# Mamba2 and feed-forward kernel: loads, scores and weight pieces of the first scan in another order

## The chip, the cores and the metric

The kernel runs on one core of one Trainium2 chip. The metric is the device time of one execution in microseconds (us), as a median of runs. Beside it stands one profiled execution with a trace of every instruction. Engines are named as in the profile: PE is TensorE's products and PEld its weight loads, DVE is VectorE, ACT is ScalarE, POOL is GpSimd, SP is SyncE, which issues most DMAs.

## The reference

A Mamba2 block over 4 batches, 8 heads, 768 positions, head size 32 and state size 16 comes first; its output, taken as 3,072 tokens of 256 values, goes through a feed-forward layer of 2,048 units.

```python
log_a = log(clip(a, 1e-6, 1))
state = 0
for c in chunks:                       # of 32 positions
    cum = cumsum(log_a[c])
    L = exp(cum[i] - cum[j]) * (i >= j)
    y = ((C @ B.T) * L) @ x + (C @ state) * exp(cum)
    state = exp(sum(log_a[c])) * state + sum_j(B_j x_j * exp(cum[-1] - cum_j))
...
h = y @ w_in                           # 3072x256 by 256x2048
out = (h * sigmoid(1.702 * h)) @ w_out # 2048x256
```

The weights w_in and w_out arrive as 64-bit floats, the other inputs as 32-bit floats.

## The kernel before, in words

Tokens go in six groups of 512. The scan works on pairs of heads and blocks of 128 positions, each split into two halves of 64. The instruction order of every engine is the order in which the program writes them: a function at the end of the program chains each engine's instructions, so nothing is rescheduled. What is written earlier on an engine runs earlier on it and holds up what follows.

**The first scan** (lines 1133 to 1199) makes the first token group. Its chain is: idle products that keep TensorE occupied (`keep_busy`, L437), masks (L545), differences of the running sums of log a (`cum`, L340 and L342, into `ab`, L551), their exponentials (L572), transposed B (`b`, L624), scores C·B (`cb`, L677, one call for each of two pairs), fanned decay rows (`rows`, L509) and their exponentials (`since`, L514), weighing the scores (L688), the state's increments (`A`, L708), `drop` (L519), the increments scaled into `steps` (L727), one scan over them on VectorE (L732), the copied state `S` (L737), then y from scores (L820) and from the state (L808), and the copy of y into the feed-forward's operand (L837). `score` calls `since_first` between its two pairs.

**Selector tiles** are made by GpSimd at the start: `same` (from which `part` is reduced), `pick`, and `whose`, which `rows` multiplies with `cum`. ACT loads a table for Ln, makes `cum` (L340), and loads the next table.

**The hidden layer of group 0** is 16 products `h` (L876), f=0 to f=15, each of two steps over 256 inputs and 512 tokens, and the profile shows 4 records of 0.43 us spacing for each f. Each needs the decoded weights of its tile f. Then come `o` products (L974) of the output layer, and from group 1 on a Strassen-like scheme (X, Y, acc).

**The weight pieces.** Weights are loaded as raw 64-bit words and decoded in `PIECES`: w_in in pieces of 2, 2, 2, 2, 4 and 4 tiles f (numbers 0 to 5), then w_out in four pieces of 4 tiles (6 to 9). `fetch(i)` issues two DMAs on SP for piece i (L180); with `held`, a one-column VectorE write (L171) makes it wait in VectorE's order. Decoding is a row of steps:

- `fields`: two VectorE operations (L192 power, L195 mantissa) on the high words
- `clamp`: two ACT operations (L203, L204) on the power
- `rounded`: one VectorE operation (L208) that adds the low words
- `join`: two VectorE operations (L219 sign into the power, L225 the product, written into `w_in` or `w_out`)

`narrow(i)` is `rounded(i)`, `fields(i+1)`, `join(i)`. A dictionary of places says after which hidden or output product a step stands: in the hidden layer of group 0 `narrow` stands at places 1, 2, 4, 6, 9, 12 for pieces 2 to 7 and the following `clamp` at 1, 2, 4, 7, 12, 15.

**Loads at the start.** On ACT's queue: two of a, four of C. On SP's: two of a, four of B, then the two of piece 0 (256 KB each), then four of x. Pieces 1 to 5 are issued after the first weighing.

**Later scans.** Two further scans stand in the output products of group 0 (place 9) and in the first step of group 1 ("H0"). There `keep_both` multiplies the increments with `part` on VectorE (L755), four operations per place.

Of the kernel before, what the change touches and what calls it, by code (L numbers as in the profile page):

```python
# [35 lines left out]
def kernel(  # L36
# [121 lines left out]
    bits, pieces = {}, {}  # L158
# [4 lines left out]
    def fetch(i, held=False):  # L163
        name, f, n = PIECES[i]
        if n == 2 and f % 4:
            t = pieces.pop(i - 1)[:, 2 * n * DM:]
        else:
            t = pieces[i] = words(f"bits{i}")
            t = t[:, :2 * n * DM]
        if held:  # L170
            nc.vector.memset(t[:, :1], 0)  # L171
        if name == "in":
            src = moe_w_in[:, 2 * f * P:2 * (f + n) * P].rearrange("(k p) e -> p k e", p=P)
            dst, src = (v.rearrange(s, h=n, e=2 * P) for v, s in (
                (t, "p (h k e) -> k p h e"), (src, "p k (h e) -> k p h e")))
        else:
            src = moe_w_out[f * P:(f + n) * P, :].rearrange("(f p) (h e) -> h p f e", p=P, h=2)
            dst = t.rearrange("p (h f e) -> h p f e", h=2, f=n)
        for k in range(2):
            nc.sync.dma_start(out=dst[k], in_=src[k])  # L180
        t = t.rearrange("p (e w) -> p e w", w=2)
        bits[i] = t[:, :, 0], t[:, :, 1]
# [5 lines left out]
    def fields(i):  # L188
        hi, cols = bits[i][1], slice(0, PIECES[i][2] * DM)
        mantissa[i] = wide.tile([P, PN], U32, tag="m", name=f"m{i}")[:, cols]  # L190
        power[i] = wide.tile([P, PN], U32, tag="p2", name=f"p2{i}")[:, cols]
        nc.vector.tensor_scalar(out=power[i], in0=hi, scalar1=0x7FF00000, scalar2=None,  # L192
                                op0=ALU.bitwise_and)

        nc.vector.tensor_scalar(out=mantissa[i], in0=hi, scalar1=0x000FFFFF,  # L195
                                scalar2=0x00100000, op0=ALU.bitwise_and, op1=ALU.bitwise_or)
# [18 lines left out]
    def join(i):  # L215

        name, f, n = PIECES[i]
        hi, m, p2 = bits.pop(i)[1], mantissa.pop(i), power.pop(i)
        nc.vector.scalar_tensor_tensor(out=p2, in0=hi, scalar=0x80000000, in1=p2,  # L219
                                       op0=ALU.bitwise_and, op1=ALU.bitwise_or)  # L220
        if name == "in":
            dst, h = w_in[:, f:f + n].rearrange("p f k e -> p (f k e)").unsqueeze(1), 1
        else:
            dst, h = w_out[:, :, f:f + n].rearrange("p c f e -> p c (f e)"), 2
        nc.vector.scalar_tensor_tensor(  # L225
            out=dst, in0=m.bitcast(FP32).rearrange("p (h e) -> p h e", h=h),
            scalar=2.0 ** -20, in1=p2.bitcast(FP32).rearrange("p (h e) -> p h e", h=h),
            op0=ALU.mult, op1=ALU.mult)
        for n in NEXT.get(i, ()):
            fetch(n)  # L230

    def narrow(i):
        rounded(i)
        if i + 1 < len(PIECES):
            fields(i + 1)
        join(i)
# [48 lines left out]
    load_first("C", [nc.scalar] * R)  # L285
    load_first("B", [nc.sync] * R)
    fetch(0)
    load(0, "x")
    load(1, "x")

# [39 lines left out]
    def fold_ident(k, engine=nc.vector):  # L330
# [8 lines left out]
                            op1=ALU.min)  # L339
    nc.scalar.activation(cum, az0, AF.Ln)  # L340
# [16 lines left out]
    def pick_a(p):  # L357
# [8 lines left out]
    same = ssd.tile([P, NH, D], FP32, tag="BT", name="same")  # L366
    nc.gpsimd.memset(same, 1.0)
    nc.gpsimd.affine_select(
        out=same, in_=same, pattern=[[-N, NH], [0, D]], compare_op=ALU.is_ge,
        fill=0.0, base=0, channel_multiplier=1)  # L370
    nc.gpsimd.affine_select(
        out=same, in_=same, pattern=[[N, NH], [0, D]], compare_op=ALU.is_ge,
        fill=0.0, base=N - 1, channel_multiplier=-1)
    pick = picker("pick", NB, 1, NH)
    whose = const.tile([32 * PG, 1 + PG, NH, N], FP32, name="whose")
    nc.gpsimd.memset(whose, 1.0)
    for i, n, head in ((0, 1, PG), (1, 2, PG), (0, 0, 1)):
        t = whose[32 * i:32 * i + 32, n:n + 1]
        nc.gpsimd.affine_select(out=t, in_=t, pattern=[[-1, 1], [-head, NH], [0, N]],
                                compare_op=ALU.is_equal, fill=0.0, base=-max(n - 1, 0),  # L380
                                channel_multiplier=1)

    part = const.tile([P, Q], FP32, name="part")
    nc.vector.tensor_reduce(
        out=part, in_=same[:, :, 0].rearrange("p (r q) -> p q r", q=Q), op=ALU.add, axis=AX.X)
# [275 lines left out]
    def score(pairs, between=lambda: None):  # L664

        cb = area(f"cb{pairs[0]}").rearrange("p r (k e) -> p r k e", k=2 * PG)
        for n, p in enumerate(pairs):
            s = st[p]
            BT, CT = s["BT"], s.pop("CT")
            s["cb"] = cb[:, :, 2 * n:2 * n + 2]  # L670
            if n:
                between()
            for k in range(2):
                for i, side in enumerate(SIDES):
                    for r in range(R):
                        rows = slice(32 * r, 32 * r + 32)
                        nc.tensor.matmul(  # L677
                            out=s["cb"][side, r, k].rearrange("p (q i) -> p q i", q=Q),
                            lhsT=BT[rows, k, side], rhs=CT[rows, k, :, side],
                            start=True, stop=True, tile_position=(32 * r, H * i),  # L680
                            skip_group_check=True)
# [57 lines left out]
    def keep_both(pairs):  # L739

        for p in pairs:
            part_of(p, range(4))
        for p in pairs:
            add_up(p, range(4))

    def part_of(p, ms):
# [4 lines left out]
        for i in range(2):  # L751
            ks = [m // 2 for m in ms if m % 2 == i]
            if ks:
                k, n = ks[0], len(ks)
                nc.vector.tensor_tensor(  # L755
                    out=new.rearrange("p (k s) (q d) -> p s k q d", s=2, q=Q)[:, i, k:k + n],
                    in0=increment[p][i][:, k:k + n].rearrange("p k (q d) -> p k q d", q=Q),
                    in1=part.unsqueeze(1).unsqueeze(3).to_broadcast([P, n, Q, D]),
                    op=ALU.mult)
# [392 lines left out]
    keep_busy(5, 0)  # L1152
# [3 lines left out]
    for r in range(R):  # L1156
        if r == R - 1:
            pads(0, busy)
# [11 lines left out]
    fields(0)  # L1170
    ends_first(0)
    ends_first(1)
    rounded(0)
    score(range(PG), since_first)
    weigh(0)
    fetch(1, held=True)
    for i in range(2, 6):
        fetch(i)
    rows_a(az, (nc.sync,))
    weigh(1)  # L1180
    drops()
    gain(range(PG))
    parts_first()
    for p in range(PG):
        since_start(p, nc.gpsimd)
    clamp(0)
# [3 lines left out]
    dense(0)  # L1190
    join(0)
    fields(1)
    clamp(1)
    table(AF.Silu)
    rounded(1)
    fields(2)
    clamp(2)
    join(1)
# [18 lines left out]
    for i, k, c in ((2, 1, 1), (3, 2, 2), (4, 4, 4), (5, 6, 7), (6, 9, 12), (7, 12, 15)):  # L1217
# [11 lines left out]
    at(in_project[0], 9, lambda: gain(pairs), lambda: score(pairs), lambda: keep_both(pairs),  # L1229
# [14 lines left out]
       lambda: since_start(n + 1), lambda: gain(later), lambda: score(later),  # L1244
       lambda: keep_both(later), lambda: weigh(n), lambda: weigh(n + 1))
# [186 lines left out]
```

## Time and profile before

| What | Value |
| --- | --- |
| Median of four runs | 351.76 us (351.21 to 352.29) |
| Profiled execution | 350.64 us |
| Its span, first to last instruction | 348.8 us |
| PE busy in the span | 342.8 us |
| DVE busy | 255.1 us |
| ACT busy | 149.8 us |
| POOL busy | 13.0 us |
| Start of the first hidden product | 18.08 us |
| Start of the hidden product f=8 | 33.16 us |

All times in the views are microseconds from the start of the span; the profiled execution is 1.84 us longer than its span. A line of the timeline gives the start, the time to the end of the last of a group, the engine, the line, the operation with its tiles and shapes, and in brackets how long the engine had been idle and what ended that. A line of the waits gives who waited for what, the sum, the number of times and the longest. In the chain of waits, each line is a step of the work that ended last, followed back from the end.

### The profile page before, as it was taken

Reading aid. Unit: us, or ns where it says so; the run is one execution under the profiler, and the core shown is the slowest. Engines: PE = TensorE matmul, PEld = TensorE weight load, DVE = VectorE, ACT = ScalarE, POOL = GpSimd, SP = SyncE. Lnnn points to the kernel's source line nnn. Section 1 sums busy time; section 2 is a strip of 40 time slices with the busy share of each in tenths; the row PEclk is TensorE's granted clock in tenths of the full one; section 3 lists DMA queues with packets and bytes.
Section 4 is the critical chain, followed back from the end, with each engine's and each line's share of the span. In section 5 each row is a group of like instructions: output and inputs, shape, how many; then the busy total and the mean of one; then the engine's idle time right before and its main releaser. Section 6 shows DMA issues by size and latency. Waiting matters only on the chain.

```text
span 348.8 us, 8109 instructions
## 1 busy us (share of the span) xinstructions
PE 342.8 (98%) x3386; PEld 274.0 (79%) x3386; DVE 255.1 (73%) x481; ACT 149.8 (43%) x334; POOL 13.0 (4%) x41
## 2 busy tenths in 40 slices
PE   8899999999999999999999999999999999999996
PEld 6643444548888888888888888888888888899996
DVE  5889999899679998739996548788454654455463
ACT  4798584005354323744342544432554321554320
POOL 8300000100000100000000000000000000000000
PEclk9999999999999999999999999999999999999999
DMA  5599899453627200435503026300000300000301
GB/s 156 121 323 217 236 204 200 85 92 66 112 54 139 45 0 9 70 89 114 103 23 54 2 75 123 62 0 3 0 4 2 60 3 0 0 2 0 62 0 61
DMA packets 89980, 25.92 MB, mean 74 GB/s; under 512 B 73432, under 2 KB 87128, under 8 KB 89944
## 3 DMA queue, kind: packets, MB, share of 16 engines
q1 hardware_dynamic: 89112, 24.88, 33.2%
q10 hardware_dynamic: 832, 0.52, 0.5%
q8 instruction: 26, 0.43, 0.5%
q14 instruction: 10, 0.08, 0.1%
HBM read 22.15 MB, written 3.24 MB: 73 GB/s over the span
## 4 chain that ended last, share of the span: by engine, by line
PE 92%; DMA 3%; DVE 2%; SPq 1%; issue 0%; ACT 0%; DVEq 0%
PE acc L1037 28%; PE X L932 19%; PE Y L942 14%; PE o L974 8%; PE acc L1044 7%; PE h L876 6%; DMA bits<-in_moe_w_in_dram 3%; PE y L820 2%; PE cb L677 2%; PE y L808 1%; SPq L180 1%; PE A L708 1%; PE busy L437 1%; PE ab L551 1%; PE ab L545 0%; DVE c L1068 0%
## 5 line engine op out<-in xcount | busy, mean ns | idle before, releaser
L937 ACT ACTIVATE ac<-X 128x256 f32<-128x256 f32 x76 | 29.1, 383 | 78.6 <-PE X L932 78.2
L1037 PE MATMUL acc<-mg,mw 128*128 128x256 f32 x192 | 54.5, 379 | 0.0
L909 ACT ACTIVATE gT<-gT 128x512 f32<-128x512 f32 (+1 forms) x76 | 39.3, 520 | 33.7 <-DVE gT L1064 33.1
L1064 DVE TENSOR_TENSOR gT<-Y,ac 128x512 f32<-128x512 f32 x38 | 26.2, 689 | 35.7 <-PE Y L942 30.4
L932 PE MATMUL X<-my,mi 128*128 128x256 f32 x152 | 45.1, 380 | 0.0
L1064 DVE TENSOR_TENSOR gT<-Y,b 128x256 f32<-128x256 f32 x38 | 15.9, 419 | 34.8 <-PE Y L942 34.8
L1037 PEld LDWEIGHTS acc<-mg,mw 128*128 128x128 f32 x192 | 36.5, 190 | 5.0
L876 PE MATMUL h<-yT,w_in 128*128 128x512 f32 (+2 forms) x108 | 35.9, 486 | 0.8 <-DVE w_in L225 0.8
L1037 PE MATMUL acc<-gT,w_out 128*128 128x256 f32 x128 | 35.5, 379 | 0.0
L876 PEld LDWEIGHTS h<-yT,w_in 128*128 128x128 f32 x108 | 18.2, 190 | 17.0 <-issue 13.9
L932 PEld LDWEIGHTS X<-my,mi 128*128 128x128 f32 x152 | 28.0, 190 | 3.8 <-ACT ac L937 0.2
L974 PE MATMUL o<-gT,w_out 128*128 128x512 f32 x64 | 28.6, 597 | 0.0
L900 DVE TENSOR_TENSOR mg<-gT 128x512 f32<-128x512 f32 x40 | 27.3, 681 | 0.0
L1037 PEld LDWEIGHTS acc<-gT,w_out 128*128 128x128 f32 x128 | 24.2, 190 | 3.4 <-ACT yT L847 0.2
L937 ACT ACTIVATE b<-X 128x256 f32<-128x256 f32 x38 | 14.6, 384 | 20.3 <-PE X L932 19.8
L932 PE MATMUL X<-yT,w_in 128*128 128x256 f32 x76 | 23.2, 389 | 0.0
L942 PE MATMUL Y<-my,mi 128*128 128x256 f32 x76 | 22.7, 381 | 0.1
L942 PE MATMUL Y<-yT,w_in 128*128 128x256 f32 x76 | 22.7, 381 | 0.0
L932 PE MATMUL X<-my,w_in 128*128 128x256 f32 x76 | 22.5, 379 | 0.0
L942 PE MATMUL Y<-yT,mi 128*128 128x256 f32 x76 | 22.4, 379 | 0.0
L974 PEld LDWEIGHTS o<-gT,w_out 128*128 128x128 f32 x64 | 11.8, 190 | 13.2 <-issue 12.8
L399 DVE TENSOR_TENSOR_SCAN L<-a,idents 128x1024 f32<-128x1024 f32 x9 | 20.5, 2277 | 0.2 <-DMA a<-scratch 0.2
(152 smaller groups left out, 543.8 us busy)
## 6 DMA issues: line engine op xcount, KB each, us to landing
a<-scratch SPq DMA_DIRECT2D x18, 256.0 KB, 5.0
bits<-in_moe_w_out_dram SPq DMA_DIRECT2D x8, 512.0 KB, 5.2
x<-in_x_dram SPq DMA_DIRECT2D x24, 128.0 KB, 3.6
out_dram<-ob SPq DMA_DIRECT2D x40, 64.0 KB, 1.9
bits<-in_moe_w_in_dram SPq DMA_DIRECT2D x8, 256.0 KB, 4.1
bits<-in_moe_w_in_dram SPq DMA_DIRECT2D x4, 512.0 KB, 9.9
b<-in_B_dram SPq DMA_DIRECT2D x20, 64.0 KB, 2.5
af<-in_a_dram SPq DMA_DIRECT2D x3, 384.0 KB
```

What stands on the lines that cost most here:

```text
L399: nc.vector.tensor_tensor_scan(out=L, data0=ra[p].rearrange("p k e -> p (k e)"), data1=idents.rearrange("p h i -> p (h i)"), initial=0.0, ...
L677: nc.tensor.matmul(out=s["cb"][side, r, k].rearrange("p (q i) -> p q i", q=Q), lhsT=BT[rows, k, side], rhs=CT[rows, k, :, side], start=Tru ...
L876: nc.tensor.matmul(out=h[:, cols], lhsT=w_in[:, f, k], rhs=yT[g][:, k, cols], start=(k == 0 and e == 0), stop=(k == NK - 1), skip_group_ch ...
L900: nc.vector.tensor_tensor(out=t[:, 0:2], in0=B[:, :, 1], in1=B[:, 0], op=ALU.subtract)
L909: nc.scalar.activation(o, i, AF.Silu, scale=GELU_SCALE)
L932: nc.tensor.matmul(out=s["X"], lhsT=lhsT, rhs=rhs, start=i == "1", stop=i == "4", skip_group_check=True)
L937: nc.scalar.activation(copy, s["X"], AF.Copy)
L942: nc.tensor.matmul(out=o, lhsT=lhsT, rhs=rhs, start=s.pop("new", False), stop=i != "5", skip_group_check=True)
L974: nc.tensor.matmul(out=o[c], lhsT=w_out[:, c, f], rhs=gT[g, f // 2][:, f % 2], start=(f == 0), stop=(f == NF - 1), skip_group_check=True)
L1037: nc.tensor.matmul(out=acc[g][0][i][:, cols], lhsT=w, rhs=h[:, cols], start=(j == 0 and k == 0 and (i, 0) in begins), stop=(j == NF // 2 - ...
L1044: nc.tensor.matmul(out=o[k] if type(o) is list else o[:, cols], lhsT=h[:, cols], rhs=w, start=(j == 0 and (i, k) in begins), stop=(j == NF ...
L1064: nc.vector.tensor_tensor(out=o, in0=v, in1=w, op=ALU.add)
```

## The change

In the first scan C's loads alternate between SP and ACT and stand ahead of B's; x's loads stand ahead of piece 0. `keep_busy` issues three products instead of five, and two small products stand before the last mask. `whose` is copied from the identity by ACT ahead of `cum`'s Ln; `same` shrinks to one column per head, and `pick` is made later. The two scores stand back to back and `since_first` comes after them and the first weighing. `fields(0)` stands behind the second weighing and ahead of the scan; `rounded(0)` stands behind the state.

Pieces 0 and 1 share one raw tile as before; `fetch(2, both=True)` loads pieces 2 and 3 by two DMAs of 512 KB. `join` can be done in parts: pieces 0, 1 and 4 are joined in two halves, and `fields(1)` is split into its two operations around the second half of `join(0)`. `clamp(6)` moves from place 7 to 8. In the later scans `keep_both` runs on ACT by eight activations per place, and `score` stands ahead of `gain` (place 9) or behind `keep_both` ("H0").

```diff
-    def fetch(i, held=False):
+    def fetch(i, held=False, both=False):
         name, f, n = PIECES[i]
-        if n == 2 and f % 4:
-            t = pieces.pop(i - 1)[:, 2 * n * DM:]
-        else:
-            t = pieces[i] = words(f"bits{i}")
-            t = t[:, :2 * n * DM]
+        n = n * (1 + both)
+        t = half.pop() if half else words(f"bits{i}")
+        if i == 0:
+            half.append(t[:, PN:])
+            t = t[:, :PN]
...
-    def fields(i):
+    def fields(i, steps=range(2)):
...
-    def join(i):
+    def join(i, parts=1, part=None):
+        for k in range(parts) if part is None else (part,):
+            name, f, n = PIECES[i]
+            n //= parts
+            f += k * n
+            cols = slice(k * n * DM, (k + 1) * n * DM)
+            hi, m, p2 = (v[:, cols] for v in (bits[i][1], mantissa[i], power[i]))
...
     def narrow(i):
         rounded(i)
         if i + 1 < len(PIECES):
             fields(i + 1)
-        join(i)
+        join(i, 2 if i == 4 else 1)
...
-    load_first("C", [nc.scalar] * R)
+    load_first("C", [nc.sync, nc.scalar] * PG)
     load_first("B", [nc.sync] * R)
-    fetch(0)
     load(0, "x")
     load(1, "x")
+    fetch(0)
...
+    whose = const.tile([32 * PG, 1 + PG, NH, N], FP32, name="whose")
+    for i, n, head in ((0, 1, PG), (1, 2, PG), (0, 0, 1)):
+        e = 32 * i + max(n - 1, 0)
+        nc.scalar.copy(whose[32 * i:32 * i + 32, n],
+                       ident[32 * i:32 * i + 32, e:e + head * NH:head].unsqueeze(2).to_broadcast(
+                           [32, NH, N]))
     nc.scalar.activation(cum, az0, AF.Ln)
...
-    same = ssd.tile([P, NH, D], FP32, tag="BT", name="same")
+    same = const.tile([P, NH], FP32, name="same")
...
-    pick = picker("pick", NB, 1, NH)
-    whose = const.tile([32 * PG, 1 + PG, NH, N], FP32, name="whose")
-    nc.gpsimd.memset(whose, 1.0)
...
+                if by_scalar:
+                    for q in range(Q):
+                        nc.scalar.activation(o[:, :, q], a[:, :, q], AF.Copy, scale=part[:, q:q + 1])
+                else:
+                    nc.vector.tensor_tensor(
...
-    keep_busy(5, 0)
+    keep_busy(3, 0)
...
-            pads(0, busy)
+            pads(2, busy)
...
-    fields(0)
     ends_first(0)
     ends_first(1)
-    rounded(0)
-    score(range(PG), since_first)
+    score(range(PG))
     weigh(0)
+    since_first()
     fetch(1, held=True)
-    for i in range(2, 6):
+    fetch(2, both=True)
+    for i in range(4, 6):
         fetch(i)
     rows_a(az, (nc.sync,))
     weigh(1)
+    fields(0)
     drops()
     gain(range(PG))
     parts_first()
     for p in range(PG):
         since_start(p, nc.gpsimd)
+    pick = picker("pick", NB, 1, NH)
     clamp(0)
     keep_first()
     dense(2)
     finish(range(PG))
-    dense(0)
-    join(0)
-    fields(1)
+    rounded(0)
+    join(0, 2, 0)
+    fields(1, (0,))
     clamp(1)
+    join(0, 2, 1)
+    fields(1, (1,))
     table(AF.Silu)
     rounded(1)
+    join(1, 2, 0)
     fields(2)
     clamp(2)
-    join(1)
+    join(1, 2, 1)
     load(PG)
...
-    for i, k, c in ((2, 1, 1), (3, 2, 2), (4, 4, 4), (5, 6, 7), (6, 9, 12), (7, 12, 15)):
+    for i, k, c in ((2, 1, 1), (3, 2, 2), (4, 4, 4), (5, 6, 8), (6, 9, 12), (7, 12, 15)):
...
-    at(in_project[0], 9, lambda: gain(pairs), lambda: score(pairs), lambda: keep_both(pairs),
+    at(in_project[0], 9, lambda: score(pairs), lambda: gain(pairs), lambda: keep_both(pairs, True),
        lambda: weigh(PG), lambda: weigh(PG + 1))
...
-       lambda: since_start(n + 1), lambda: gain(later), lambda: score(later),
-       lambda: keep_both(later), lambda: weigh(n), lambda: weigh(n + 1))
+       lambda: since_start(n + 1), lambda: gain(later), lambda: keep_both(later, True), lambda: score(later),
+       lambda: weigh(n), lambda: weigh(n + 1))
```

## The prediction, made before the run

> **What bounds the kernel now.** I read the page's busy shares first, then TensorE's waits over the first 60 us, then the chain of waits from the start, then the timelines of each engine up to 50 us.
>
> ```profile
> PE 342.8 (98%) x3386; PEld 274.0 (79%) x3386; DVE 255.1 (73%) x481; ACT 149.8 (43%) x334; POOL 13.0 (4%) x41
> ```
>
> TensorE is busy for 98%, so only its idle time, and work taken off it, can pay. The list of its waits is short:
>
> ```profile
> PE busy L437 <- DVE ones L296: 1.2, 1, 1.2
> PE h L876 <- DVE w_in L225: 0.8, 1, 0.8
> PE b L624 <- ACT L L572: 0.5, 1, 0.5
> PE y L808 <- DVE S L737: 0.4, 1, 0.4
> ```
>
> The columns are microseconds, times, longest. The last long one is `h` L876 on `w_in` L225. It ends at 33.16, and after it the same list, asked for 50 us to the end, is empty: TensorE runs product against product. So whatever the change gains or loses up to 33.16 moves the whole remaining stream, and nothing later can give it back. The chain up to that point:
>
> ```profile
> 12.34 1.26 DVE L L688 x2
> ...
> 18.40 10.81 DMA bits<-in_moe_w_in_dram
> 29.33 0.69 DVE p L192
> 30.02 0.60 DVE m L195
> 30.62 1.14 DVE p L219
> 31.79 1.24 DVE w_in L225
> 33.16 3.67 PE h L876 x8
> ```
>
> Columns: start, time, what. Hidden product f=8 waits for the first w_in piece of four tiles, and VectorE decodes that (L192 to L225) in one unbroken row. The third view is the front of the timeline (start, time, engine, line, shapes, in brackets the idle time ahead):
>
> ```profile
> 1.21 3.56 PE L437 MATMUL busy<-ones 128*128 128x192 f32 x10 [1.21 <-DVE ones L296]
> 4.44 0.42 ACT L340 ACTIVATE cum<-az 128x256 f32<-128x256 f32 x1 [0.79 <-DVE az L338]
> 4.89 0.69 DVE L342 TENSOR_TENSOR_SCAN cum<-carry,cum 128x256 f32<-128x256 f32 x1 [0.48 <-ACT cum L340]
> 6.41 0.90 PE L551 MATMUL ab<-cum,pick 32*64 32x128 f32 x32
> 7.90 0.69 PE L551 MATMUL ab<-cum,pick 32*64 32x128 f32 x32
> 11.64 0.66 ACT L514 ACTIVATE since<-rows 128x256 f32<-128x256 f32 x2 [1.17 <-PE rows L509]
> 14.62 1.23 DVE L732 TENSOR_TENSOR_SCAN steps<-drop,steps 128x512 f32<-128x512 f32 x1
> 18.08 14.23 PE L876 MATMUL h<-yT,w_in 128*128 128x512 f32 x32
> ```
>
> `cum` is ready at 5.58, but L551, which uses it, starts at 6.41: until then TensorE is still in its idle products and the masks. From there run `ab`, `b`, the scores, `rows`, `since`, drops, the scan at 14.62, and y; the hidden layer starts at 18.08, which is 2.23 after the scan ends.
>
> **The change, part by part.**
>
> *Fewer idle products.* Five become three, 10 records become 6. Spacing is 0.32, so the masks end about 1.28 earlier, near 5.2 (two tiny new pads among them cost no more than 0.1). L551 then waits for `cum`: 5.58 plus about 0.07 is 5.65, which is 0.76 earlier. The same 32 products take 0.90 at 6.41 and 0.69 at 7.90, and single starts lie 0.21 apart before 6.92 and 0.11 after. If that change of pace stays at 6.92, 0.76 us at half pace is worth about 0.47 later: `b`, at 9.70, goes to about 9.23. It follows ACT's L572, whose first bank follows the products and moves with them.
>
> *Selectors.* Three ScalarE copies stand ahead of `cum`'s Ln. No row shows a 32x128 copy; L727's 128x128 steps are 0.25 apart, L737's 128x256 copy takes 0.66. At 0.14 to 0.27 each they take 0.4 to 0.8 from 3.65 on, where ACT is idle 0.79: they end at 4.05 to 4.45 against 4.44. That costs 0 to 0.1, which I take as 0. POOL loses L376/L379, the large `same` and `pick` from its early row; its products CT (7.80) only gain slack.
>
> *Loads.* C now shares SP and ACT, so the four B issues on SP are joined by two of C, but the two bits issues leave: ahead of x stand two issues where two stood. x starts near 5.47 as before, and x (from L708 at 12.16) is not late. B's last issue ends near 5.45 instead of 4.45; with the 2.2 to 2.7 of its landings before it is there by 7.7 to 8.1, and its transpose (L612, 1.02) ends by 8.7 to 9.1, just ahead of `b` at 9.23: cover 0.1, and what lacks there delays all that follows. Piece 0's bits go behind x; that is rival A.
>
> *Scores together, rows after them.* Now `rows` L509 runs after the second score. `since` came 1.94 after `b` (11.64 − 9.70); it now comes after 0.59 + 0.49 + 0.57 + 0.73 = 2.38 (b, two scores, rows to ACT). With `b` at 9.23 that is 11.61, against 11.64: what the front gains, this order takes back. So the scan stays at 14.6 and h starts at 18.05, 0.03 earlier. L688 (weigh), which needs both scores, moves from 12.34 to about 11.07 and ends its second half at 13.42; the held fetch, released by it, moves from 13.62 to about 12.3.
>
> *Fields(0), clamp(0), rounded(0).* Before, fields(0) stood at 9.08 and L208 at 11.14, beside the scan's chain. Now L192/L195 stand between weigh(1) and the scan, and L208 behind S. They take 0.77, so 13.34 to 14.1, inside the 0.5 that VectorE has before 14.62. Cost 0, if the bits have landed by 13.85.
>
> *Decode in halves.* This is the real gain. From h's start TensorE itself needs 0.53 + 31 × 0.43 = 13.86 to f=8: 31.94. It got there at 33.16, so 1.22 is wait (0.23 of it at f=2, about 1.0 at f=8). VectorE's row from S to piece 4 decides. Its steps from start to start are: 512 columns 0.34, 0.34, 0.60 to 0.72, 0.72, 0.61; 1,024 columns 0.60, 0.60, 1.12, 1.25, 1.14; for a half join of 256 columns I go by L1064's 128x256 (0.42 long): 0.45 to the dependent second step, 0.34 to the next. Adding up from S at 15.88: rounded(0) 16.19, half 0 of piece 0 at 17.66 (f=0 needs it at 18.05), half 1 at 18.79 (f=1: 19.9), piece 1's first half at 20.97 (f=2: 21.62, before 21.63), its second 22.44 (f=3: 23.3), piece 2 at 25.05 (f=4: 25.06), piece 3 at 28.2 (f=6: 28.7), first half of piece 4 at 31.84. With the 0.14 from ready to product and some restart at f=4, f=8 runs at 32.15. That is 33.16 − 32.15 = 1.01. Bounds: 0.7 if each half costs 0.1 more and f=4 waits 0.2; 1.22 if no wait is left.
>
> *Pieces 2 and 3 in one load.* Eight issues on SP instead of ten, 0.47 to 0.59 each, starting 1.3 earlier. But piece 2 now needs the whole megabyte. Before, both pieces had landed by 21.85; 1.3 earlier is 20.5, wanted by fields(2) at 20.9: cover 0.4. Piece 4 is wanted at 25.6 (landed by 25.3 before), piece 5 at 29.2 (29.20 before). If the cover goes, its lateness moves f=4 one for one.
>
> *After 33 us.* keep_both goes to ScalarE: eight activations per place instead of four VectorE products of 0.81; ACT is 43% busy and waits for PE there, S has 3.2 to 3.4 cover (70.65 against L808 at 73.87), and Be of pair 5 (84.60 against 85.34) gains VectorE time. Score ahead of gain only swaps TensorE work. clamp(6) at f=8 has its piece ready 2.0 us before its product (46.95 against 48.96), less the 1.0 that TensorE comes earlier and 0.3 for the split join. Cost 0 each; without these covers the first would cost 0.8 per place.
>
> Sum: 0.03 + 1.01 = 1.04 less, out of 350.64 (span 348.8 and 1.84 around it). The median of the runs is 351.76, so 1.12 above the profiled one; the same difference gives 350.7.
>
> **The rivals.**
>
> *A, slower: the scan waits for piece 0.* fields(0) stands ahead of the scan on VectorE, and its bits are now queued behind x, issued until 10.72 (or 9.8, without the 0.94 of bits issues ahead). Its second transfer is issued at 10.3 to 11.2. Piece 1's pair, issued at 13.62 and 14.03, landed 2.8 and 3.9 later; the page's median for a 512 KB bits load is 5.2. So it lands between 13.1 and 16.4, wanted by 13.85. Behind the wait queue scan, S, y and the whole hidden layer, one for one. Landing at 14.9 eats the gain; landing after 15.95 is slower by over 0.3%. Against: the nearest rows, 2.8 to 3.9, end at 15.1, 352.0. For: x goes in small packets (the page counts 73,432 of 89,980 under 512 B) on the same engines just ahead. Its far end, 2.55 late, gives 353.3; I put it at 16.0, 352.9.
>
> *B, the pace of TensorE rises later.* Fewer idle products leave it resting about 0.45 before L551. If the spacing halves only after the scores, L551's second half, b and scores pay up to 1.4; with the order above up to 0.4 of the sum of 1.04 remains: 351.4. For: the pace changed 5.7 us after the first idle product. Against: the granted clock reads 1.00 in every stretch from 1.2 to 100, and the rest is short.
> On this the Trainium skill, "TensorE: Matmul & The Clock Gate", Part 1, says that the clock doubles after a busy window of about 3.4 us that runs freely, not after a number of products; that speaks against taking busy work away. An estimate by that page puts a missed window at up to half of 3.4, 1.7 us later, and the time at 352.4; the trace shows the halved spacing, but not what sets it.
>
> *C, better.* The pace rises earlier, or `rows` slips in sooner, so that the scan starts 0.4 earlier, and the halves end all waits: 1.22 + 0.4 gives 350.1.
>
> *D, it doesn't bite.* Merged pieces 2 and 3, or 4, land late and the wait only moves from f=8 to f=4: gain 0 to 0.4, 351.5.
>
> **How the numbers follow.** The main case has 0.48, A 0.17, B 0.09, C 0.18, D 0.08. A measurement can tell about 0.3%, which is 1.06 us: faster means below 350.7, on which the main case sits, so half of it (0.24) counts as faster, the rest as same. Faster: 0.24, 0.18 of C, and 0.01 each of B and D: 0.44. Slower: 0.12 of A, 0.02 of B: 0.14. Same: 0.42. The range takes C from 349.9 on and reaches up through B and D and the nearer part of A, to 352.4; 0.14 lies above, 0.05 below.
>
> **What would show it.** L551 at 5.6 to 5.7; the scan at 14.5 to 14.7; h starting within 0.1 of 18.05; no wait on `w_in` over 0.2 at f=8, and f=8 at 32.1 to 32.2; then the same stream, 1.0 earlier. It is wrong if `p` L192 waits for `bits` past 13.9 with the scan behind it (A), if products of 0.21 spacing last beyond 8 (B), if h waits at f=4 (D), or if any new TensorE wait appears after 33 us.

## The result, and the profile after

| | before | after |
| --- | --- | --- |
| Median of runs | 350.99 us (78 runs, 349.67 to 353.95) | 352.45 us (54 runs, 350.32 to 356.3) |
| Profiled execution, its span | 350.64, 348.8 us | 353.02, 351.1 us |
| First scan on VectorE starts | 14.62 us | 15.11 us |
| Hidden layer starts | 18.08 us | 18.69 us |
| Hidden product f=8 | 33.16 us | 34.23 us |
| Output product of group 0 starts | 48.96 us | 49.95 us |

The ratio is 1.0037, with a 95% interval of 1.0024 to 1.005: the change makes the kernel slower by about 1.3 us. Faster by about 1.0 us was predicted.

The page of the kernel after has the same matmuls, a TensorE as full as before, and more ScalarE work (154.1 against 149.8 us):

```profile
PE 343.7 (98%) x3386; PEld 273.5 (78%) x3386; DVE 253.7 (72%) x479; ACT 154.1 (44%) x353; POOL 10.8 (3%) x37
...
PEclk9989999999999999999999999999999999999999
```

TensorE's waits over the first 60 us (who waits for what, sum, number of times, longest):

```profile
PE y L826 <- issue: 1.4, 1, 1.4
PE busy L440 <- DVE ones L305: 1.2, 1, 1.2
PE b L627 <- ACT L L575: 0.5, 1, 0.5
PE y L826 <- ACT steps L728: 0.2, 1, 0.2
PE ab L554 <- DVE part L390: 0.2, 1, 0.2
```

The wait of `h` on `w_in`, 0.8 in the list of before, is gone. That does not yet speak for the halves: TensorE came to f=8 at 34.23, 1.1 after VectorE had its weights ready (33.14), because it had been slowed, as shown below. A wait of 1.4 has come in `y`, with "issue" as its cause, which means that no engine and no data transfer released it. TensorE's timeline in the same execution:

```profile
5.73 0.69 PE L554 MATMUL ab<-cum,pick 32*64 32x128 f32 x32 [0.15 <-DVE part L390]
...
8.81 0.65 PE L627 MATMUL b<-ident,Bt 128*128 128x128 f32 x4 [0.46 <-ACT L L575]
...
14.17 1.00 PE L826 MATMUL y<-L,x 64*32 64x64 f32 x77 [0.17 <-ACT steps L728]
16.61 0.48 PE L826 MATMUL y<-L,x 64*32 64x64 f32 x33 [1.44 <-issue]
...
18.69 19.13 PE L882 MATMUL h<-yT,w_in 128*128 128x512 f32 x40
```

The front came earlier than before: `ab` at 5.73 instead of 6.41 (5.65 was forecast), and `b` at 8.81 instead of 9.70 (9.23 was forecast). Still the hidden layer starts 0.61 later than before. VectorE's timeline says what lies between:

```profile
14.38 0.48 DVE L194 TENSOR_SCALAR p<-bits 128x512 uint32<-128x512 uint32 x1 [1.37 <-DMA bits<-in_moe_w_in_dram]
...
15.11 1.21 DVE L733 TENSOR_TENSOR_SCAN steps<-drop,steps 128x512 f32<-128x512 f32 x1
16.35 0.39 DVE L738 COPY S<-steps 128x256 f32<-128x256 f32 x1
...
19.04 0.43 DVE L194 TENSOR_SCALAR p<-bits 128x512 uint32<-128x512 uint32 x1 [0.90 <-DMA bits<-in_moe_w_in_dram]
```

`fields(0)` stands ahead of the scan and waits 1.37 for piece 0 to land. ScalarE had the scan's operand `steps` done at about 14.1, so the scan could have started near 14.15, and it starts at 15.11:

```profile
12.86 1.25 ACT L728 ACTIVATE steps<-A,part 128x128 f32<-128x128 f32 x4
```

Piece 1 is late too, by 0.90. What follows is shown in the busy time by stretch (columns: stretch, microseconds, busy time and count of PE, PEld, DVE, ACT, POOL, granted clock, DMA share, GB/s):

```profile
18.00:22.00 4.00, 4.00 (x30) 1.87 (x25) 3.00 (x8) 3.74 (x7) 0.00 (x0) 0.62 1.09 361
22.00:26.00 4.00, 4.00 (x10) 1.86 (x9) 3.93 (x10) 3.92 (x8) 0.00 (x0) 0.95 1.08 298
```

The granted clock averages 0.62 over the first four microseconds; the trace records it as one stretch at half speed, from 19.00 to 22.41. The records of the first hidden products lie 0.85 us apart there, not 0.43. Before, the same two stretches were granted 1.00. From f=0 to f=8 TensorE takes 15.54, which is 1.68 more than the 13.86 that the prediction gives for full pace without waits; before, the waits on the way were 1.22. So f=8 comes at 34.23, 1.07 later than before (0.61 + 1.68 − 1.22). Later waits add the rest up to the span's 2.3. After 50 us, where the kernel before had no wait in the list, two stand:

```profile
PE X L938 <- ACT ac L943: 0.3, 1, 0.3
PE y L826 <- issue: 0.3, 1, 0.3
```

One profile is one draw. Of the 54 runs after, 17 show a mean granted clock of 0.995 or less, like this one, with a median of 353.77; the other 37 have 351.82, still 0.8 above before. (One stretch of 3.41 us at half speed lowers the mean over 351 us by 0.005, so 0.995 is one such stretch and 0.99 two.) So the half-speed stretch is part of the loss and not all of it, and experiments had to say what lies behind both.

### The profile page after: what moved, and what is told of

Its sections match the earlier page's. It is cut to its first block, busy times and chain, and to the rows that moved or that the text cites. A ratio compares the mean times of both kernels' runs of the same rounds, so it can differ in the third digit from the quotient of the medians.

```text
span 351.1 us, 8129 instructions
## 1 busy us (share of the span) xinstructions
PE 343.7 (98%) x3386; PEld 273.5 (78%) x3386; DVE 253.7 (72%) x479; ACT 154.1 (44%) x353; POOL 10.8 (3%) x37
## 4 chain that ended last, share of the span: by engine, by line
PE 95%; DVE 1%; ACT 1%; issue 1%; DMA 1%; SPq 0%; DVEq 0%
PE acc L1043 28%; PE X L938 18%; PE Y L948 14%; PE h L882 10%; PE o L980 8%; PE acc L1050 7%; PE y L826 3%; PE cb L678 2%; PE y L814 2%; PE A L709 1%; PE ab L554 1%; DMA az<-in_a_dram 1%; DVE c L1074 0%; ACT steps L728 0%; DVE u L1074 0%
## 5 line engine op out<-in xcount | busy, mean ns | idle before, releaser
L882 PE MATMUL h<-yT,w_in 128*128 128x512 f32 (+2 forms) x108 | 37.1, 502 | 0.0
L882 PEld LDWEIGHTS h<-yT,w_in 128*128 128x128 f32 x108 | 19.0, 196 | 16.7 <-issue 14.3
```

The costliest lines, as they stand in the source:

```text
L882: nc.tensor.matmul(out=h[:, cols], lhsT=w_in[:, f, k], rhs=yT[g][:, k, cols], start=(k == 0 and e == 0), stop=(k == NK - 1), skip_group_ch ...
```

## The experiments

Five chips were used; each kernel is compared with runs of the kernel before on its own chip. "After" or "before" says which kernel an edit was made to.

**First batch: which part loses?**

e1, after, with piece 0 ahead of x again:

```diff
     load_first("B", [nc.sync] * R)
+    fetch(0)
     load(0, "x")
     load(1, "x")
-    fetch(0)
```

> The changed kernel with piece 0 loaded ahead of x again; all else as changed. Wait theory (the scan L733 stands behind fields(0), which waited until 14.38 for piece 0): the wait of 1.37 on VectorE goes, the scan starts at 14.1 to 14.3 instead of 15.11 unless the increments now wait for x, h starts 0.6 to 1.0 earlier, TensorE's rest of 1.44 ahead of y L826 goes, ratio to the kernel before 0.997 to 1.000. Rival, clock theory (the half pace at 18.7 comes of fewer idle products at the start): the half pace stays, ratio 1.002 to 1.004. Rival, x late: the increments A wait for x by about 1 us instead, scan at 14.9 to 15.3, ratio 1.002 to 1.004.

Ratio 1.0038 (1.0014 to 1.0063). The wait for piece 0 went, and x took its place:

```profile
13.35 0.35 PE L709 MATMUL A<-x,Be 64*32 64x64 f32 x16 [0.51 <-DMA x<-in_x_dram]
```

The scan starts at 15.15, as in after. So the order of x and piece 0 on SP is not the cause by itself: with two of C's issues ahead of them on that queue, the one that stood second was late both times. None of the 12 runs was at a low clock, and the loss is that of after: the low clock is not needed for it.

e2, after, with five idle products and no pads:

```diff
-    keep_busy(3, 0)
+    keep_busy(5, 0)
...
-            pads(2, busy)
+            pads(0, busy)
```

> The changed kernel with five idle products and no pads, as before the change; all else as changed. Clock theory: no stretch of halved product spacing after 18 us, granted clock 1.00 in nearly all runs, ratio 0.998 to 1.001, although the front starts about 0.5 to 0.8 later. Wait theory: the scan still waits for piece 0 until about 14.4, so the later front costs nothing more and the ratio stays at 1.002 to 1.005.

Ratio 1.0042 (1.0018 to 1.0066); `ab` is back at 6.41, and the low clock came in 2 of 12 runs. The number of idle products does not decide the loss.

e3, before, with the halves alone (`join` in two parts for pieces 0, 1 and 4, `fields(1)` split):

```diff
-    join(0)
-    fields(1)
+    join(0, 2, 0)
+    fields(1, (0,))
     clamp(1)
+    join(0, 2, 1)
+    fields(1, (1,))
...
+    join(1, 2, 0)
     fields(2)
     clamp(2)
-    join(1)
+    join(1, 2, 1)
```

> The kernel before with only the decode in halves: join of pieces 0, 1 and 4 in two parts, fields(1) split, the order of the decode steps of the change; loads, idle products, selectors, scores and the later scans as before. If the halves are worth what the prediction gave (1.0 us at f=8): f=8 at 32.1 to 32.3 instead of 33.16, ratio 0.996 to 0.998. Rival (the wait only moves to f=4 or f=6, or the later fields of the next piece fall behind): f=8 at 32.8 or later, ratio 0.999 to 1.001.

Ratio 0.998 (0.9959 to 1.0001), none of 12 runs at a low clock. This is the only kernel whose interval lies almost wholly below 1, and in its profile the hidden layer runs with one short wait:

```profile
5.57 0.69 PE L558 MATMUL ab<-cum,pick 32*64 32x128 f32 x32 [0.16 <-DVE part L394]
...
17.41 7.13 PE L883 MATMUL h<-yT,w_in 128*128 128x512 f32 x16
24.73 10.54 PE L883 MATMUL h<-yT,w_in 128*128 128x512 f32 x24 [0.18 <-ACT p L205]
```

By this the halves bring 0.7 us, with an interval (0.0 to 1.4) that touches zero; the loss lies in the other parts. The first line shows something else: with five idle products, as before, `ab` starts at 5.57 here and not at 6.41. How early the front comes differs from run to run.

e4, after, with the later scans as before:

```diff
-    at(in_project[0], 9, lambda: score(pairs), lambda: gain(pairs), lambda: keep_both(pairs, True),
+    at(in_project[0], 9, lambda: gain(pairs), lambda: score(pairs), lambda: keep_both(pairs),
...
-       lambda: since_start(n + 1), lambda: gain(later), lambda: keep_both(later, True), lambda: score(later),
+       lambda: since_start(n + 1), lambda: gain(later), lambda: score(later), lambda: keep_both(later),
```

> The changed kernel with the later scans as before: keep_both by VectorE and the order of gain and score. Later theory (the waits at 80.8 and 120.9 in the trace after come of the eight activations on ScalarE): these two gaps of 0.44 and 0.51 go, ratio 1.000 to 1.002. Rival (they are late transfers and a late instruction fetch, whatever engine does keep_both): the gaps come and go, ratio 1.003 to 1.005.

Ratio 1.0038 (1.0011 to 1.0066), 6 of 12 runs at a low clock: not the cause. f4, the counterpart, puts these later scans into before (the diff above, the other way round):

> The kernel before with the later scans alone as changed: keep_both by ScalarE in both places, score ahead of gain at place 9 and behind keep_both in H0. If they cost nothing, as the prediction had it: no TensorE wait over 0.2 after 60 us, ratio 0.999 to 1.001. Rival (the increments wait for CsT behind the scores, or ScalarE is late for X near 120): waits of 0.3 to 1.5 at 65 to 67 or near 120, ratio 1.001 to 1.003.

Ratio 0.9999 (0.9973 to 1.0025): they cost nothing. This kernel's first 33 us hold the same instructions as before's, and its hidden layer tells more:

```profile
17.76 3.70 PE L881 MATMUL h<-yT,w_in 128*128 128x512 f32 x8
21.62 14.25 PE L881 MATMUL h<-yT,w_in 128*128 128x512 f32 x32 [0.16 <-DVE w_in L225]
```

The one wait listed is 0.16 at f=2, and f=8 stands inside the second row, at 32.20, without one. The wait of 0.8 at f=8 in the profile before, on which the gain was reckoned, is as good as absent here with nothing changed in that stage; in g3, below, it is too. It was one draw of when a transfer landed.

**Second batch: the start of the scan.**

f1, after, with a longer filler ahead of y:

```diff
-    dense(2)
+    dense(4)
```

> The changed kernel with four instead of two filler products (L1154) ahead of the y products, in the time in which TensorE rests for the scan anyway. Clock theory (the slow stretch of the hidden layer comes of TensorE's rests between 13 and 17 us): the granted clock is 1.00 in nearly all runs, where a third of the runs of the changed kernel had 0.989 to 0.995, and the ratio falls from 1.0037 to about 1.001 to 1.002. Rival (the clock falls for another reason, or the wait for piece 0 is all): clocks as in the changed kernel, or clean clocks and a ratio still at 1.003 to 1.005.

Ratio 1.0027 (0.9994 to 1.006), 3 of 12 at a low clock, where after has 17 of 54: no help is shown. Its profile says something on the rest in y, which is taken up in the part on why the prediction was wrong.

f2, before, with piece 0 late, on SP and on VectorE:

```diff
-    fetch(0)
     load(0, "x")
     load(1, "x")
+    fetch(0)
...
-    fields(0)
...
-    rounded(0)
...
     weigh(1)
+    fields(0)
     drops()
...
     finish(range(PG))
+    rounded(0)
```

> The kernel before with rival A's edits alone: x ahead of piece 0, fields(0) behind the second weighing, rounded(0) behind the state; no halves, everything else as before. Wait theory: the scan starts at 14.8 to 15.2, the first decoded piece 0.6 later from the state on, f=8 at 34.0 to 34.6, ratio 1.003 to 1.005, and some runs with a granted clock under 0.996. Rival (the wait for piece 0 is small beside the front's own variation): scan at 14.0 to 14.6, ratio 1.000 to 1.002.

Ratio 1.0025 (0.9996 to 1.0054), 5 of 12 at a low clock. Piece 0 was there in time in its profile and the scan started at 14.31, but VectorE then waited 0.94 for the bits of piece 2, and TensorE meets that in the hidden layer:

```profile
22.62 14.16 PE L876 MATMUL h<-yT,w_in 128*128 128x512 f32 x32 [0.93 <-DVE w_in L225]
```

h1 puts f2's edits onto the halves of e3:

> The kernel before with the halves (as e3) and rival A's edits (x ahead of piece 0, fields(0) behind the second weighing, rounded(0) behind the state, as f2) together, nothing else. Load-order theory (these edits hold up the scan, lengthen the decode chain and bring the slow clock in a third of the runs, 0.9 us, and the halves save 0.7): scan at 14.3 to 15.1, low clocks in 3 to 6 runs of 12, ratio 1.000 to 1.002. Rival (with halves there is slack enough): no low clocks, ratio 0.997 to 0.999.

Ratio 1.0046 (1.002 to 1.0073), against 0.998 for e3: by these two the late piece 0 costs about 2.3 us (1.1 to 3.5) on top of the halves, though f2 alone showed 0.9. Against h3, which has the halves and ran on the same chip, it is 1.3. So this group of edits costs time, and the halves do not make up for it; how much is less sure.

f3, after, with C on ScalarE's queue, piece 0 first, and `fields(0)` and `rounded(0)` in their old places, which should have mended that cause:

```diff
-    load_first("C", [nc.sync, nc.scalar] * PG)
+    load_first("C", [nc.scalar] * R)
     load_first("B", [nc.sync] * R)
+    fetch(0)
     load(0, "x")
     load(1, "x")
-    fetch(0)
...
+    fields(0)
     ends_first(0)
     ends_first(1)
+    rounded(0)
```

> The changed kernel without rival A's edits: C on ACT's queue and piece 0 ahead of x, fields(0) and rounded(0) at their old places; fewer idle products, selectors, scores together, merged pieces 2 and 3, halves and the later scans as changed. Wait theory: scan at 13.9 to 14.5, no wait on w_in over 0.3, h from 17.4 on, ratio 0.997 to 1.000. Rival (scores together, merged pieces or the later scans cost as much): ratio 1.002 to 1.004.

Ratio 1.0073 (1.0043 to 1.0103): worse. Pieces 2 and 3, merged, landed at 23.64:

```profile
25.43 1.96 PE L882 MATMUL h<-yT,w_in 128*128 128x512 f32 x4 [1.82 <-DVE w_in L232]
```

g2 takes f3 with pieces 2 and 3 apart, and g1 takes after with them apart:

```diff
-    fetch(2, both=True)
-    for i in range(4, 6):
+    for i in range(2, 6):
         fetch(i)
```

> The kernel of f3 (the changed one with piece 0 early) with pieces 2 and 3 loaded apart as well. If the merged load alone made f3 slow: piece 2 lands at 19 to 20.5 instead of 23.64, the wait of 1.8 for w_in goes, ratio 0.998 to 1.001 instead of 1.0073. Rival (the front is slow by itself, with cum late behind ScalarE's selectors and C issues, and rows behind the scores): ratio 1.002 to 1.005.

> The changed kernel with pieces 2 and 3 loaded apart again (four transfers of 256 KB instead of two of 512 KB); all else as changed. Merge theory (piece 2's wait for the whole megabyte is a main loss): fields(2) never waits, ratio falls from 1.0037 to about 1.000 to 1.002. Wait theory (the merged load was just in time, the loss is the scan behind piece 0 and the clock after it): ratio stays at 1.003 to 1.005.

g2: 1.007 (1.0044 to 1.0097); g1: 1.004 (1.0013 to 1.0067). Loading the pieces apart helps neither. In g2's profile the wait of 1.8 is gone, and its time is no better. Something else made every version that had grown out of after slow.

h4, after, with piece 0 issued on ScalarE's queue behind Ln:

```diff
     load(0, "x")
     load(1, "x")
-    fetch(0)
...
     nc.scalar.activation(cum, az0, AF.Ln)
+    fetch(0, queue=nc.scalar)
```

> The changed kernel with piece 0's two transfers issued on ACT's queue behind cum's Ln (beside SP's issues of x) instead of behind x on SP; all else as changed. Load-order theory (the loss is that x and piece 0 follow each other on one queue): piece 0 there by 11, fields(0) right behind the second weighing at 13.0 to 13.2, scan at 14.1 to 14.3, low clocks rare, ratio 0.997 to 1.000. Rival (the engines are the limit and x comes later instead, or the loss is elsewhere): A waits for x by over 0.5 or the scan is at 14.3 but the ratio stays at 1.002 or more.

Ratio 1.0078 (1.0049 to 1.0106). Piece 0 no longer waits, but the 1.5 us of issues stand ahead of ScalarE's table load, and `b` waits 1.2 instead of 0.5.

**Third batch: parts of the change alone, on before.**

g3, before, with the two scores together and `since_first` behind `weigh(0)`; g4, e3 with three idle products and the two pads (e2's diff, the other way round); h3, e3 and g3 together. The edit of g3:

```diff
-    score(range(PG), since_first)
+    score(range(PG))
     weigh(0)
+    since_first()
```

> The kernel before with only the scores together: both scores, the first weighing, then rows and since; the held load is released earlier by this. The prediction's sum: since 0.44 later against b, scan 0.3 to 0.5 later, the load 0.5 to 1.2 earlier; f=8 later by up to 0.5, ratio 1.000 to 1.0015. Rival (the decode chain takes its start from the loads and not from the scan): f=8 not later, ratio 0.998 to 1.000.

> The kernel of e3 (before, with the decode in halves) with three idle products and two pads instead of five. If fewer idle products bring the slow clock by themselves: a third of the runs at a granted clock of 0.989 to 0.995, ratio 1.000 to 1.002. If the slow clock needs the late rests of the changed kernel: clock 1.00 in nearly all runs, L551's counterpart at 5.6 to 5.8 in every draw, ratio 0.996 to 0.998, at least as good as e3's 0.998.

> The kernel before with the halves and with the scores together (g3's edit), nothing else; a candidate that may beat both. If the halves' gain stands and the scores together cost nothing at f=8 (g3 had 0.9993): ratio 0.996 to 0.998. If the later rows take what the prediction gave (0.44): ratio 0.998 to 1.000.

Ratios: g3 0.9993 (0.9965 to 1.002), g4 0.9993 (0.996 to 1.0026), h3 1.001 (0.9984 to 1.0036). None of the three parts loses measurably. In g4 the front was 0.39 earlier than before's (`ab` at 6.02), but by f=8, at 33.16, TensorE had given it all back in two waits for `w_in` (0.55 and 0.66), in spite of the halves. At 67 us it lost more:

```profile
PE A L715 <- DVE CsT L669: 1.7, 1, 1.7
```

There VectorE is late because it stood 1.56 at 57 us for the bits of a w_out piece, ahead of the second group's `CsT` in its order. From 18 to 60 us the DMA engines are busy for 0.92 to 0.98 of the time in the profiles of before, e1, g4 and h2, so products that come earlier meet data that do not.

h2, before, with the remaining part alone: `whose` by ScalarE's three copies, `same` as a small tile, `pick` made late, C on SP and ScalarE.

```diff
-    same = ssd.tile([P, NH, D], FP32, tag="BT", name="same")
+    same = const.tile([P, NH], FP32, name="same")
```

> The kernel before with the selectors by ScalarE (whose copied, same small, pick late) and C shared by SP and ACT, nothing else; piece 0 stays ahead of x, which is two issues later for it. If the prediction's 0 for both holds: x still in time, ratio 0.999 to 1.001. Load-order theory (x has no room either): the increments A wait for x by 0.5 to 1.0, scan at 14.6 to 15.3, ratio 1.000 to 1.003, granted clock 1.00.

Ratio 1.0099 (1.0061 to 1.0136), the slowest of all, with its scan only 0.44 late:

```profile
PE A L702 <- DVE CsT L656: 2.9, 1, 2.9
PE h L870 <- DVE w_in L225: 2.3, 2, 1.4
```

Both hang on transfers. Behind the wait for `CsT`, near 70 us, stands VectorE: it sat idle for 3.59 until a piece of w_out landed, at a place where the kernel before waits for no piece:

```profile
60.31 0.69 DVE L192 TENSOR_SCALAR p<-bits 128x1024 uint32<-128x1024 uint32 x1 [3.59 <-DMA bits<-in_moe_w_out_dram]
```

The part that I had priced at 0 is the dearest of those tried on before.

**Fourth batch: why the selectors cost.** The diff line above moves `same` from a pool where it shared a slot to the pool of constants, where it takes 32 bytes per partition. All tiles placed behind the constants, the targets of the loads among them, move by 32 bytes; added up from the tile sizes in the program, each rounded up to 32 bytes, the first tile of raw weights starts at a multiple of 256 bytes before, and 32 bytes behind one after. (The traces hold no addresses.) Over the 12 kernels that have a shift, the transfers take 122.8 to 130.0 us per DMA engine, and a packet of 1,024 bytes takes 54 to 57 ns on average; over the 8 without it, 118.6 to 122.9 us and 51 to 54 ns. These ranges touch. The slow packets part the two groups clearly: the median packet of 1,024 bytes takes 46 ns in all 20 profiles, but 26 to 31% of them take over 48 ns in the 12, and 8 to 12% in the 8.

i2 does nothing else: before, with one small constant 32 bytes longer. No instruction differs.

```diff
-    part = const.tile([P, Q], FP32, name="part")
+    part = const.tile([P, 16], FP32, name="part")[:, :Q]
```

> The kernel before with one edit: the tile part takes 64 bytes of each partition instead of 32, so that all tiles behind the constants stand 32 bytes off a multiple of 64; no instruction differs. Address theory: 1,024-byte packets 54 to 57 ns, transfers 124 to 130 us per DMA engine, waits on w_in or on CsT in the first 70 us, ratio 1.003 to 1.009. Rival (no effect of the address): packets 51 to 54 ns, ratio 0.998 to 1.002.

Ratio 1.0062 (1.0031 to 1.0093), which is 2.2 us (1.1 to 3.3) for a shift of 32 bytes. The page's row of the main DMA queue (packets, MB, share of the 16 engines' span) has the same packets and bytes as before, at 35.0% where before has 33.2% of a shorter span, so 123.9 us instead of 115.8 (114.7 to 118.9 in the eight profiles without the shift). The first row here is that of the engines:

```profile
PE 346.1 (98%) x3386; PEld 276.3 (78%) x3386; DVE 255.5 (72%) x481; ACT 149.5 (42%) x334; POOL 12.9 (4%) x41
...
q1 hardware_dynamic: 89112, 24.88, 35.0%
...
bits<-in_moe_w_in_dram SPq DMA_DIRECT2D x4, 512.0 KB, 11.4
```

The median landing of the 512 KB pieces is 11.4 us (9.9 before). VectorE's and ScalarE's own work took no longer than before (255.1 and 149.8 there), so it is not their reading of shifted tiles that costs; TensorE's 346.1 against 342.8 holds its half-speed stretch. The low clock is not the whole loss either: seven of the ten runs are at full clock, and their median is 354.50. TensorE's timeline, and one stretch of the busy table, show the same pattern as in after, only stronger:

```profile
18.41 0.74 PE L820 MATMUL y<-L,x 64*32 64x64 f32 x33 [2.60 <-issue]
```

```profile
18.00:22.00 4.00, 3.59 (x90) 3.31 (x90) 2.21 (x5) 0.86 (x3) 0.00 (x0) 0.50 0.85 247
```

i1 is after, with `same` at 64 bytes instead of 32, to see whether a shift by 64 restores the transfers:

```diff
-    same = const.tile([P, NH], FP32, name="same")
+    same = const.tile([P, 2 * NH], FP32, name="same")[:, :NH]
```

> The changed kernel with one edit: the tile same takes 64 bytes of each partition instead of 32, so that all tiles allocated behind the constants, the targets of every transfer among them, stand on multiples of 64 bytes again, as before the change. Address theory: in the ten kernels run so far with the selectors edit these tiles stand 32 bytes off, their 1,024-byte packets took 54 to 57 ns and the transfers together 122.8 to 130.0 us per DMA engine, against 51 to 54 ns and 118.6 to 122.9 in the eight without it. Then here: 51 to 54 ns, 119 to 122 us, ratio 0.998 to 1.001. Rival (the loss is piece 0 behind x alone, and the packets follow from the order of the loads): packets and total as in the changed kernel, ratio 1.003 to 1.005.

Ratio 1.0042 (1.0016 to 1.0069). It does not:

```profile
q1 hardware_dynamic: 89240, 25.02, 34.7%
```

A 1,024-byte packet takes 57 ns on average here, and 26% take over 48 ns. So the theory as it stood, that a multiple of 64 is enough, failed. The targets then stand 64 bytes off a multiple of 256; that 256 is what counts is a reading made after this run, and the version that brings them back to such a multiple was not run.

The Trainium skill, "DMA: Bandwidth & Descriptors", section "How a descriptor splits into AXI transactions", says that a descriptor is split into transactions of 256 bytes, that a transaction has to start on a multiple of 256, and that a descriptor which starts off it costs extra beats. The runs agree in direction: shifts of 32 and of 64 bytes both give more slow packets, though the median packet stays at 46 ns. The page words the rule for addresses that are read; these are addresses that are written, and no run here shows the price on both sides apart.

## Why the prediction was wrong

**What held.** L551 runs at 5.73 (5.65 forecast). The copies for `whose` end in time: Ln starts at 4.53 instead of 4.44. The merged load of pieces 2 and 3 landed at 21.90, just ahead of its use. The later scans are free, as said, now shown by f4.

**The step that failed: Selectors, "which I take as 0".** This is the largest error. I costed the instructions and not the tile. Moving `same` between pools moved the targets of all loads, and i2 shows that 32 bytes alone cost 2.2 us (1.1 to 3.3); h2, which adds the copies and C's two queues, lost 3.5 (2.1 to 4.8), and that these add anything to the shift is not shown. The diff line was there to read; its effect on every address behind it wasn't looked for. No rival covered it.

**"Cost 0, if the bits have landed by 13.85".** They landed at 14.28 in after's profile. Rival A, which had 0.17, named this mechanism and its place, and gave 13.1 to 16.4 for the landing. By its own price, one for one, 14.28 costs 0.43 and leaves 0.6 of the gain, so it does not explain a slower kernel by itself. f2 and h1, which have no shift, show the late piece 0 as a loss of its own: 0.9 (−0.1 to 1.9) alone, 1.6 (0.7 to 2.6) together with the halves.

**Halves, 1.01.** e3 measured 0.7 (0.0 to 1.4), and g4 and h3, which have them too, lie at 0.9993 and 1.001. The term came from a wait in a single profile. f4 and g3, with the same decode as before, come to f=8 with 0.57 and 0.47 of waits on the way where before has 1.22, and e3 with 0.40. "Nothing later can give it back" failed too: e1, g1 and g4 wait 1.3 to 1.7 at 67 us, behind a late piece of w_out.

**Fewer idle products, 0.76 at the front.** The number came out, but it was reckoned from one draw. The prediction let the pace of TensorE rise at 6.92, where it rose in the profile before. In the profiles with five idle products it rises between 4.17 (e3) and 7.39 us (i2), and `ab` starts anywhere from 5.57 to 6.42; with three, `ab` follows `cum` in all ten profiles. So the term is worth 0 to 0.8, by the draw.

**Rival B, the clock.** Right that the clock mattered, wrong on where and why. With three idle products the pace at the front was full from the first `ab` on. The drop comes at 19 us, behind rests of TensorE among the small products of y. The runs with a mean granted clock of 0.995 or less, by group:

| Kernels | Runs at a low clock |
| --- | --- |
| before, beside all experiments | 3 of 143 |
| no shift, piece 0 early (e3, f4, g3, g4, h3) | 1 of 60 |
| no shift, piece 0 late (f2, h1) | 8 of 21 |
| shifted (after and eleven others) | 51 of 169 |

The number of idle products does not sort them (g4, with three: 1 of 12; e2, with five: 2 of 12). Nor is every shifted kernel hit (e1: none of 12).

The Trainium skill, "TensorE: Matmul & The Clock Gate", Part 1, puts the return to half speed after an idle window of about 3.4 us. Here half-speed stretches of 3.41 (after, i1, e4) and 6.83 us (i2) followed rests among the small products of y, the longest of which were 1.44, 2.18, 0.62 and 2.60 us, all shorter than that window. But h1 rested 0.87 in y, and f3 1.82 among full-size products, without such a stretch. So half speed can follow shorter rests, and their length alone does not decide it; what the gate counts is not shown.

**The rest in y.** It has one place in TensorE's instruction stream: ahead of the 96th of the 128 products, after 706 recorded instructions, in each of the 14 profiles of other kernels that have it. f1 has four more products ahead of y, and there it stands ahead of the 91st, after 705:

```profile
14.10 1.12 PE L826 MATMUL y<-L,x 64*32 64x64 f32 x90
15.87 0.63 PE L826 MATMUL y<-L,x 64*32 64x64 f32 x38 [0.65 <-issue]
```

So it goes with the count of instructions and not with the data. In all 20 profiles a 16 KB block of TensorE's instructions is fetched ahead of that place, and the product there starts 2.2 to 3.0 us after the fetch begins: the fetch begins at 13.26 in before, which has no rest, at 14.13 in after, 15.01 in i1 and 15.40 in i2. TensorE waited for its instructions, and long where the fetch came late. What makes the fetch late, in the midst of the weight transfers, was not tried by itself.

**What stays open.** The parts do not add: they end in the same waits for transfers. Kernels without the shift and with piece 0 early lie between 0.998 and 1.001; every kernel with either of the two lies between 1.0025 and 1.0099. The shift alone is enough for a loss of after's size; the late piece 0 is clear of zero only beside the halves. How after's 1.3 us divide between them is not settled, since after was not run with its targets back on a multiple of 256. No version is shown to beat the kernel before; e3 comes nearest.

## What to carry to other kernels

A new tile is an edit of the memory map: before costing the instructions of a change, list which tiles' addresses move, and whether the targets of large loads leave a multiple of 256 bytes (32 and 64 bytes off were both slow here). When the DMA engines are full, a moved load is paid for by whatever is queued behind it, and a gain on the compute side is handed back at the next transferred operand. A wait of 1 us in one profile is a draw, not a price, and so is the moment at which TensorE's pace rises: see whether it is there in a second profile of the same stage before building a sum on it.

## What the hardware showed that was not expected

- A 32-byte shift of all tiles behind the constants, the load targets among them, with no other difference, lengthened the main queue's transfers to 123.9 us per engine (114.7 to 118.9 in the eight profiles without a shift) and the kernel by 0.62% (0.31 to 0.93). The median packet of 1,024 bytes stayed at 46 ns; those over 48 ns went from 10 to 26%.
- After rests of 0.6 to 2.6 us in a stage of 64-column products, the granted clock stood at 0.5 for 3.41 us (after, i1, e4) or 6.83 us (i2). At the front of the kernel before, the view by stretches reads 1.00 from 1.2 us on while products lie twice as far apart: the trace's record of the granted clock begins only at 6.92, where the pace rises, and the view counts the time ahead of it as full speed.
- TensorE rested at a fixed count of instructions, behind the fetch of a 16 KB block, for up to 2.60 us.
- Three copies of 32x128 on ScalarE took 0.90 us, just past the bound of 0.4 to 0.8 taken from its other rows.
